# Channel attention on one core: new load pieces in the first pass, and another order of the first stores and reads of the second

## The chip, the cores and the metric

The kernel runs on one core of a Trainium2 chip. The core's engines are TensorE (PE in the profile; its weight loads are PEld), VectorE (DVE), ScalarE (ACT), GpSimd (POOL) and SyncE (SP). Here SP issues all reads from device memory and ACT issues all stores; both go to the core's 16 DMA engines. The metric is device time in microseconds: before the change a median of 733.99 us over 3 runs (733.06 to 737.35). Less is better.

## The reference

`x` has 384 x 384 pixels of 384 channels in bfloat16, 113.25 MB; `w1` is 384 x 96 and `w2` is 96 x 384. Cut to what matters:

```python
xf = x.reshape(B, H * W, C)
gap = jnp.mean(xf, 1)          # mean of each channel
gmp = jnp.amax(xf, 1)          # maximum of each channel
h_a = relu(gap @ w1)
h_m = relu(gmp @ w1)
scale = sigmoid(h_a @ w2 + h_m @ w2)
return x * scale[:, None, None, :]
```

Nothing can be stored before all of `x` has been read once: the scale depends on every pixel.

## The kernel before

The 147,456 pixels lie as 1,152 rows on each of 128 partitions; a row is one pixel's 384 channels, 768 bytes on a partition and 98,304 bytes over all of them. A block of n rows gives each partition n pixels that lie together in memory. All amounts below are in rows.

The first pass reads all 1,152 rows and makes two things of them: running maxima in an accumulator `acc` of eleven rows (DVE, function `larger`, line 311), and sums by TensorE with a column of ones (`sums`, line 274). The second pass multiplies every row by the scale (`multiply`, line 430) and stores it. What doesn't stay on the chip has to be read a second time: 804 rows in nineteen blocks (`AGAIN`) and the accumulator's eleven.

Three slots of 44 rows (`x_88`, `x_89`, `x_90` in the profile; slots 0, 1 and 2) take the loads. `FILLS` names in order what goes into them: a fill has packed pairs (16 rows each) and plain pieces, and the fills go round the slots. Nine pairs, 144 rows, are packed by ACT and PE into three quarters of their size in `room` (function `pack`, lines 316 to 349; ACT lines 321, 324, 339, 341, 344 and 346, PE line 334) and stay there; in the second pass `unpack` (lines 457 to 479, ACT line 464, DVE lines 467 and 470) restores them. The last loads stay as they are: `STAYING`, 44 rows in each slot in the pieces named, 35 rows in `room` itself (`ROOM_PIECES`, loaded ahead of slot `ROOM_LOADS`), and ten in `late` (`LATE_PIECES`, placed among the loads of slot `LATE_AT[0]` after `LATE_AT[1]` of its pieces). Sixteen rows are kept in PSUM. While packing goes on, the first rows of `room` are its scratch, so that the room's loads wait for the last packing.

SP issues the first pass's loads in the order of the list (line 369). A load waits until DVE, PE and, for a pair, ACT have done with the rows that stood in its place; those behind it on SP wait too. `FOLDS` says with how many loads left the accumulator is folded to six and to three rows, so that little is left to fold after the last load; from then on the maxima go in operations of at most three rows (`PARTS`).

Between the passes come the last folds, the means, the transposes of the maxima, the two small products and the sigmoid (lines 297 to 425), and the accumulator's rows are read again (`refill`, line 410).

The second pass has an order written out by hand for SP, ACT and DVE. `order` starts with the three slots; the room is put in at place `ROOM_TURN`. For each block in turn `put` multiplies it and stores it, in the pieces of `FIRST_STORES` for the first ones and whole for the rest; the accumulator's two stores come ahead of piece `ACC_STORES_AT` of the first block. `read_into` takes the next block of `AGAIN` into a slot, in the pieces of `FIRST_READS` for the first two, and adds it to the order. Before the change slots 0 and 1 are read into after two blocks have been put (`LEAD`), slot 2 after four. SP issues these reads (line 454), each when the store of the rows in its place has landed. From the fifth block on, one packed group is unpacked after each.

Of the kernel before, what the change touches and what calls it, by code (L numbers as in the profile page):

```python
# [19 lines left out]
NS = 3  # L20
# [34 lines left out]

PSUM_PIECES = (4, 12)
FILLS = (
    ((16,), ()), ((), (44,)), ((), (44,)), ((16,), ()), ((), (44,)), ((), (44,)),
    ((16,), ()), ((), (44,)), ((), (44,)), ((16,), ()), ((), (44,)), ((), (44,)),
    ((16,), ()), ((), (44,)), ((), (44,)), ((16,), ()), ((), (43,)), ((), (40,)),  # L60
    ((), (36,)), ((), (36,)), ((16,), (27,)), ((), (28,)), ((), (28,)), ((16,), (26,)),
    ((), (24,)), ((), (23, 21)), ((16,), (16,)), ((), (16,)),
)
ROOM_PIECES = (10, 9, 5, 6, 5)
STAYING = ((17, 15, 12), (11, 11, 11, 11), (6, 4, 3, 4, 3, 6, 3, 3, 3, 6, 3))
ROOM_LOADS = 2
LATE_AT = (2, 1)
LATE_PIECES = (5, 5)

FOLDS = {7: 6, 1: 3}  # L70

AGAIN = (44,) * 18 + (12,)
FIRST_STORES = ((1, 2, 3, 4, 4, 6, 8, 8, 8), (8, 8, 9, 9, 10), (10, 11, 14))
FIRST_READS = ((8, 8, 8, 10, 10), (44,))
LEAD = 2
ROOM_TURN = 2
ACC_STORES_AT = 3
ACC_STORES = ((6, 11), (0, 6))
UNPACK_FROM = 4
# [6 lines left out]
def kernel(  # L86
# [20 lines left out]
    def part(ap, block, lo, hi):  # L107

        first, n = block
        return ap[first * P:(first + n) * P, :].rearrange("(p n) c -> p n c", n=n)[:, lo:hi, :]  # L110
# [103 lines left out]
    def packed_place(k):  # L214

        if k < EARLY:
            return early_b, k * PACKED
        if k < N_PACK - EARLY:
            return packed_b, k * PACKED
        return packed_b, (k - N_PACK + EARLY) * PACKED  # L220
# [8 lines left out]
    done, k = A, 0  # L229
    for i, (packs, pieces) in enumerate(FILLS):  # L230
        buf, at = slots[(i - len(FILLS)) % NS], 0
        for m in packs:
            assert m == PAIR
            block, j = packed_place(k)
# [10 lines left out]
    def pieces_of(block, pieces, buf):  # L245
        j = 0
        for m in pieces:
            loads.append((block, j, j + m, buf, j, ()))
            j += m
        assert j == block[1]  # L250

    for s, pieces in enumerate(STAYING):
        if s == ROOM_LOADS:
            pieces_of(room_b, ROOM_PIECES, room)
        n = len(loads)
        pieces_of(stay_b[s], pieces, slots[s])
        if s == LATE_AT[0]:
            j = 0
            for i, m in enumerate(LATE_PIECES):
                loads.insert(n + LATE_AT[1] + i, (late_b, j, j + m, late, j, ()))  # L260
                j += m
# [95 lines left out]
    def fold(n, to):  # L357
        while n > to:
            h = min(n // 2, n - to)
            larger(acc[:, 0:h, :], acc[:, 0:h, :], acc[:, n - h:n, :])  # L360
            n -= h
        return n
# [3 lines left out]
    for i, (block, lo, hi, buf, at, groups) in enumerate(loads):  # L366
# [14 lines left out]
        if i == len(PSUM_PIECES):  # L381
# [5 lines left out]
            continue  # L387
        if n_loads - i in FOLDS:
            width = fold(width, FOLDS[n_loads - i])
            parts, turn = PARTS[width], 0  # L390
        j = 0
# [36 lines left out]
    def multiply(dst, src):  # L428
        n = dst.shape[1]
        nc.vector.tensor_tensor(  # L430
            out=dst, in0=src, in1=scale_bc.unsqueeze(1).to_broadcast([P, n, C]), op=ALU.mult
        )
# [6 lines left out]
    def put(block, buf, pieces, acc_at=None):  # L439
        j = 0  # L440
        for i, m in enumerate(pieces):
            if i == acc_at:
                put_acc()
            rows = buf[:, j:j + m, :]
            multiply(rows, rows)
            nc.scalar.dma_start(out=part(orr, block, j, j + m), in_=rows)
            j += m
        assert j == block[1]
# [8 lines left out]
    def unpack(k):  # L457
        low, code = planes(k)
        j = packed_place(k)[1]
        rows = room[:, j:j + PACKED, :]  # L460
        words = rows.bitcast(U16)
        bits = acc[:, 0:PACKED, :].bitcast(U16)
        more = acc[:, PACKED:PACKED + n_grp, :].bitcast(U16)
        nc.scalar.activation(out=words, in_=low, func=ACT.Copy, bias=float(HIGH))  # L464

        def field(out, shift, op, mask):
            nc.vector.tensor_scalar(out=out, in0=code, scalar1=shift, scalar2=mask, op0=op, op1=ALU.bitwise_and)  # L467

        def add(out, a, b):
            nc.vector.tensor_tensor(out=out, in0=a, in1=b, op=ALU.bitwise_or)  # L470

        for r in range(GROUP - 1):
            field(bits[:, r * n_grp:(r + 1) * n_grp, :], 4 * r, ALU.logical_shift_left, HIGH_BITS)
        last = bits[:, PACKED - n_grp:PACKED, :]
        field(more, 12, ALU.logical_shift_left, 0x8000)
        field(last, 4, ALU.logical_shift_right, 0x0700)
        add(last, last, more)
        add(words, words, bits)
        multiply(rows, rows)

    order = [(b, s) for s, b in enumerate(stay_b)]
    order.insert(ROOM_TURN, (room_b, None))
    stores, reads = list(FIRST_STORES), list(FIRST_READS)
    n_turns = len(order) + len(again)

    def read_into(s):
        if s is None or not again:
            return
        block = again.pop(0)
        get(block, slots[s], reads.pop(0) if reads else (block[1],))  # L490
        order.append((block, s))

    room_left, j = [], EARLY * PACKED
    for m in ROOM_STORES:
        room_left.append((j, j + m))
        j = (j + m) % packed_b[1]
    assert j == EARLY * PACKED

    def put_room(count):
        for _ in range(count):  # L500
            lo, hi = room_left.pop(0)
            nc.scalar.dma_start(out=part(orr, packed_b, lo, hi), in_=room[:, lo:hi, :])
# [5 lines left out]
    while k < len(order):  # L508
        block, s = order[k]
        buf = room if s is None else slots[s]  # L510
        put(block, buf, stores.pop(0) if stores else (block[1],), None if k else ACC_STORES_AT)
        k += 1
        if k == LEAD:
            for j in range(k):
                read_into(order[j][1])
        elif k > LEAD:
            read_into(s)
        if k > UNPACK_FROM and unpacked < N_PACK:
            unpack(unpacked)
            unpacked += 1  # L520
            if unpacked == EARLY:
                nc.scalar.dma_start(out=part(orr, early_b, 0, early_b[1]), in_=room[:, 0:early_b[1], :])
        if k == n_turns - 2:
            put_room(1)
        elif k == n_turns - 1:
            put_room(2)
            multiply(late, late)
            nc.scalar.dma_start(out=part(orr, late_b, 0, LATE_ROWS), in_=late)
# [48 lines left out]
```

## Time and profile before

| | |
|---|---|
| Median of 3 runs | 733.99 us (733.06 to 737.35) |
| The profiled run's own time | 734.48 us |
| Its span, from the first instruction to the last | 732.6 us |
| Read from and written to device memory | 193.51 MB, 113.25 MB |
| Mean rate over the span | 419 GB/s |
| DVE busy | 556.5 us (76%) |
| ACT busy | 250.8 us (34%) |
| PE busy, weight loads | 162.8 us (22%), 52.0 us (7%) |
| First multiply of the second pass starts | 280.36 us |

In the profile a group of instructions is named by its line, engine, operation and what it writes and reads; "x8" is how many, then come the busy time, the mean of one in ns, and the idle time of the engine before them with what ended it. In the timeline the first two numbers of a row are its start and its length in us, and the bracket at the end is the idle time ahead of it. The page's slices cut the span in 40 parts of 18.3 us. The stretches give, for a window in us, the busy time and number of instructions of PE, PEld, DVE, ACT and POOL, the granted clock of PE, the DMA share and the rate in GB/s. In the rows on DMAs the last number is the median time in us from issue to landing, and KB is the size of one; 4224 KB are 44 rows, 1536 KB are sixteen.

### The profile page before, as it was taken

The page shows a single profiled execution, that of the slowest core. Times are in us where ns is not written, and L with a number is a line of the kernel's source. Part 1 is how long each engine was busy: PE and PEld are TensorE (multiplying, and loading weights), DVE is VectorE, ACT ScalarE, POOL GpSimd, SP SyncE. Part 2 cuts the span into 40 slices and gives each one's busy share as a digit, 9 for nine tenths or more (in the row PEclk, how much of TensorE's full clock was granted, in tenths as well). Part 3 has the DMA queues.
Part 4 walks back from the last instruction along what each step waited for, and adds up shares of the span by engine and source line. Part 5 has one row for each costly group of instructions (what it writes and reads, how often), then busy time and mean ns, then how long its engine had stood idle before and what let it go on. Part 6 is the DMA issues. An engine that isn't in the chain of part 4 may idle for free.

```text
span 732.6 us, 3124 instructions
## 1 busy us (share of the span) xinstructions
PE 162.8 (22%) x1069; PEld 52.0 (7%) x1078; DVE 556.5 (76%) x422; ACT 250.8 (34%) x135; POOL 0.7 (0%) x6
## 2 busy tenths in 40 slices
PE   3664656554756561000000000000000000000000
PEld 0221212111211120000000000000000000000000
DVE  6689989899999998979276777277667666667930
ACT  4998889853997400002011011011110011111100
POOL 0000000000000000000000000000000000000000
PEclk9968878677675755555555555555555555555555
DMA  9999999999999988999999999999999999999997
GB/s 378 440 431 414 431 415 412 400 426 427 427 424 422 417 329 306 386 442 425 437 439 424 435 436 441 421 437 440 424 437 437 423 437 439 423 437 427 434 438 339
DMA packets 19391, 306.95 MB, mean 419 GB/s; under 512 B 2512, under 2 KB 3120, under 8 KB 8368
## 3 DMA queue, kind: packets, MB, share of 16 engines
q1 hardware_dynamic: 12896, 193.52, 62.5%
q10 hardware_dynamic: 6480, 113.25, 36.2%
q8 instruction: 8, 0.13, 0.1%
q14 instruction: 7, 0.06, 0.0%
HBM read 193.51 MB, written 113.25 MB: 419 GB/s over the span
## 4 chain that ended last, share of the span: by engine, by line
DMA 58%; DVE 34%; issue 2%; ACT 0%; SPq 0%; PE 0%; DVEq 0%; ACTq 0%
DMA x<-in_x_dram 37%; DMA out_dram<-x 21%; DVE hole L311 20%; DVE x L430 12%; DVE room L430 1%; DVE hole L430 1%; ACT room L464 0%; SPq L369 0%; DVE room L470 0%; DVEq L535 0%; PE bank_a L424 0%; ACT scale_bc L425 0%; DVE small L419 0%; PE bank_a L418 0%; PE bank_a L422 0%
## 5 line engine op out<-in xcount | busy, mean ns | idle before, releaser
L430 DVE TENSOR_TENSOR x<-x,scale_bc 128x16896 bf16<-128x16896 bf16 (+9 forms) x34 | 191.5, 5660 | 94.6 <-DMA x<-in_x_dram 93.5
L311 DVE TENSOR_TENSOR hole<-hole,x 128x1920 bf16<-128x1920 bf16 (+2 forms) x211 | 235.7, 1191 | 20.0 <-DMA x<-in_x_dram 18.6
L464 ACT ACTIVATE room<-room 128x3072 uint16<-128x3072 uint8 x18 | 49.7, 2763 | 360.2 <-DVE x L430 309.4
L274 PE MATMUL bank_a<-x,small 128*1 128x512 bf16 (+1 forms) x816 | 92.7, 481 | 49.4 <-DMA x<-in_x_dram 48.6
L334 PE MATMUL bank_b<-room 128*128 128x512 bf16 x153 | 59.9, 526 | 51.9 <-ACT room L324 22.4
L321 ACT CAST room<-x 128x3072 bf16<-128x3072 uint8 x18 | 48.7, 2750 | 45.1 <-DMA x<-in_x_dram 45.1
L339 ACT COPY room<-x 128x3072 uint8<-128x3072 uint8 x18 | 49.3, 2737 | 0.0
L470 DVE TENSOR_TENSOR room<-room,hole 128x3072 uint16<-128x3072 uint16 x18 | 31.6, 1758 | 23.0 <-ACT room L464 23.0
L341 ACT ACTIVATE room<-room,w_sb 128x6144 uint8<-128x6144 bf16 x9 | 48.7, 5407 | 0.0
L430 DVE TENSOR_TENSOR room<-room,scale_bc 128x3072 bf16<-128x3072 bf16 (+3 forms) x21 | 38.9, 1861 | 0.6
L274 PEld LDWEIGHTS <-small 128*1 128x1 bf16 x861 | 29.1, 95 | 131.8 <-issue 116.0
L467 DVE TENSOR_SCALAR hole<-room 128x768 uint16<-128x768 uint16 x90 | 25.7, 353 | 0.0
L346 ACT ACTIVATE room<-room,w_sb 128x3072 bf16<-128x3072 uint16 x9 | 25.7, 2853 | 0.0
L334 PEld LDWEIGHTS <-room 128*128 128x128 bf16 x162 | 19.0, 119 | 90.9 <-issue 85.7
L344 ACT ACTIVATE room<-bank_b 128x512 uint16<-128x512 f32 x27 | 15.9, 590 | 1.7 <-PE bank_b L334 1.7
L324 ACT ACTIVATE room<-x 128x1536 bf16<-128x1536 bf16 x9 | 13.3, 1478 | 0.0
L470 DVE TENSOR_TENSOR hole<-hole 128x768 uint16<-128x768 uint16 x18 | 10.0, 558 | 0.6
L299 ACT COPY w_sb<-bank_a 65x128 f32<-65x128 f32 x2 | 0.5, 262 | 25.3 <-PE bank_a L274 24.8
L311 DVE TENSOR_TENSOR hole<-hole,room 128x1920 bf16<-128x1920 bf16 (+2 forms) x7 | 7.6, 1152 | 0.0
L379 DVE COPY kept_ps<-x 128x768 uint32<-128x768 uint32 (+1 forms) x2 | 3.5, 1760 | 4.2 <-DMA x<-in_x_dram 4.2
L274 PE MATMUL bank_a<-room,small 128*1 128x512 bf16 (+1 forms) x27 | 4.1, 543 | 4.2 <-DMA room<-in_x_dram 4.2
L311 DVE TENSOR_TENSOR hole<-hole 128x1920 bf16<-128x1920 bf16 (+2 forms) x6 | 4.9, 823 | 0.1
(46 smaller groups left out, 29.8 us busy)
## 6 DMA issues: line engine op xcount, KB each, us to landing
x<-in_x_dram SPq DMA_DIRECT2D x27, 4224.0 KB, 24.4
out_dram<-x ACTq DMA_DIRECT2D x19, 4224.0 KB, 24.0
x<-in_x_dram SPq DMA_DIRECT2D x11, 1536.0 KB, 12.2
x<-in_x_dram SPq DMA_DIRECT2D x2, 3456.0 KB, 16.7
out_dram<-room ACTq DMA_DIRECT2D x2, 3072.0 KB, 31.4
x<-in_x_dram SPq DMA_DIRECT2D x2, 2688.0 KB, 16.7
x<-in_x_dram SPq DMA_DIRECT2D x4, 1056.0 KB, 11.4
out_dram<-room ACTq DMA_DIRECT2D x1, 4224.0 KB, 29.5
```

The source lines that it names most:

```text
L274: nc.tensor.matmul(sum_ps[q * QP:q * QP + 1, 0:g * P], lhsT=ones_bf[:, 0:1], rhs=rows[:, :, q * P:(q + 1) * P], start=(summed == 0), stop= ...
L311: nc.vector.tensor_tensor(out=out, in0=a, in1=b, op=ALU.max)
L321: nc.scalar.copy(out=lanes[:, h], in_=halves[:, h, :, :, 1].rearrange("p (w g) c -> p w (g c)", g=n_grp))
L334: nc.tensor.matmul(pack_ps, lhsT=diag[:, w, :], rhs=flat(src)[:, i * 512:(i + 1) * 512], start=(w == 0), stop=(w == len(WEIGHTS) - 1),)
L339: nc.scalar.copy(out=planes(k + i)[0], in_=halves[:, i, :, :, 0])
L341: nc.scalar.activation(out=flat(test).bitcast(U8), in_=flat(high), func=ACT.Abs, bias=middle, scale=1.0 / STEP)
L344: nc.scalar.activation(out=code[:, i * 512:(i + 1) * 512], in_=pack_ps, func=ACT.Copy, bias=-OFFSET)
L346: nc.scalar.activation(out=flat(test), in_=flat(test).bitcast(U16), func=ACT.Square, bias=good, accum_out=flags[:, k // 2:k // 2 + 1],)
L430: nc.vector.tensor_tensor(out=dst, in0=src, in1=scale_bc.unsqueeze(1).to_broadcast([P, n, C]), op=ALU.mult)
L464: nc.scalar.activation(out=words, in_=low, func=ACT.Copy, bias=float(HIGH))
L467: nc.vector.tensor_scalar(out=out, in0=code, scalar1=shift, scalar2=mask, op0=op, op1=ALU.bitwise_and)
L470: nc.vector.tensor_tensor(out=out, in0=a, in1=b, op=ALU.bitwise_or)
```

## The change

Only constants and the condition that starts the reads change; the work and the bytes read and stored are the same.

In the first pass most fills with a pair now have a plain piece as well, of 12 to 28 rows; there are 25 fills instead of 28, with the same nine pairs and 804 plain rows. All pairs now go into slot 2, and it is refilled every third time. The room, the staying rows and the late rows come in other pieces; the late rows are one piece of ten and are read among the loads of slot 1 instead of slot 2. The accumulator is folded to six rows with nine loads left instead of seven.

In the second pass the room is stored second, after slot 0, instead of third. The first block goes in seven pieces that begin with four rows, instead of nine that begin with one; slot 1 goes in three pieces instead of five, slot 2 in two (20 and 24) instead of whole. No read starts before three blocks have been put; then slot 1 is read into first, in pieces of 20 and 24, and slot 0 after it, whole.

```diff
 FILLS = (
-    ((16,), ()), ((), (44,)), ((), (44,)), ((16,), ()), ((), (44,)), ((), (44,)),
-    ((16,), ()), ((), (44,)), ((), (44,)), ((16,), ()), ((), (44,)), ((), (44,)),
-    ((16,), ()), ((), (44,)), ((), (44,)), ((16,), ()), ((), (43,)), ((), (40,)),
-    ((), (36,)), ((), (36,)), ((16,), (27,)), ((), (28,)), ((), (28,)), ((16,), (26,)),
-    ((), (24,)), ((), (23, 21)), ((16,), (16,)), ((), (16,)),
+    ((16,), ()), ((), (40,)), ((), (44,)), ((16,), (28,)), ((), (44,)), ((), (44,)),
+    ((16,), (28,)), ((), (43,)), ((), (27,)), ((16,), (27,)), ((), (44,)), ((), (44,)),
+    ((16,), (28,)), ((), (36,)), ((), (40,)), ((16,), (20,)), ((), (36,)), ((), (32,)),
+    ((16,), (28,)), ((), (27,)), ((), (28,)), ((16,), (24,)), ((), (23, 21)), ((), (20,)),
+    ((16,), (12, 16)),
 )
-ROOM_PIECES = (10, 9, 5, 6, 5)
-STAYING = ((17, 15, 12), (11, 11, 11, 11), (6, 4, 3, 4, 3, 6, 3, 3, 3, 6, 3))
+ROOM_PIECES = (8, 6, 5, 6, 5, 5)
+STAYING = ((16, 14, 14), (11, 11, 11, 6, 5), (4, 4, 3, 3, 6, 6, 3, 3, 6, 3, 3))
 ROOM_LOADS = 2
-LATE_AT = (2, 1)
-LATE_PIECES = (5, 5)
+LATE_AT = (1, 3)
+LATE_PIECES = (10,)
 
-FOLDS = {7: 6, 1: 3}
+FOLDS = {9: 6, 1: 3}
 
-FIRST_STORES = ((1, 2, 3, 4, 4, 6, 8, 8, 8), (8, 8, 9, 9, 10), (10, 11, 14))
-FIRST_READS = ((8, 8, 8, 10, 10), (44,))
-LEAD = 2
-ROOM_TURN = 2
+FIRST_STORES = ((4, 4, 4, 7, 8, 8, 9), (10, 12, 13), (13, 15, 16), (20, 24))
+FIRST_READS = ((20, 24), (44,))
+FIRST_INTO = (2, 0)
+ROOM_TURN = 1
...
-        if k == LEAD:
-            for j in range(k):
+        if k == NS:
+            for j in FIRST_INTO:
                 read_into(order[j][1])
-        elif k > LEAD:
+        elif k > NS:
             read_into(s)
```

`FIRST_INTO` counts places in `order`, which then holds slot 0, the room, slot 1 and slot 2: place 2 is slot 1, place 0 is slot 0.

## The prediction

> **What bounds the kernel now.** I read the page's slices first, then stretches of them, then the waits, and last DVE and the loads in the first pass.
>
> ```profile
> span 732.6 us, 3124 instructions
> ...
> GB/s 378 440 431 414 431 415 412 400 426 427 427 424 422 417 329 306 386 442 425 437 439 424 435 436 441 421 437 440 424 437 437 423 437 439 423 437 427 434 438 339
> ...
> DMA 58%; DVE 34%; issue 2%; ACT 0%; SPq 0%; PE 0%; DVEq 0%; ACTq 0%
> ```
>
> Except at the turn between the passes (slices 15 to 17) and at both ends, the transfers run at 400 to 440 GB/s; the chain that ended last is DMA and DVE alone. The bytes are the same after the change, so only stretches below the best rate can give time back. The next lines are such stretches; their last two columns are DMA share and GB/s.
>
> ```profile
> 20.00:150.00 130.00, 78.42 (x489) 25.18 (x495) 114.32 (x98) 116.38 (x60) 0.00 (x0) 0.77 1.00 418
> 150.00:240.00 90.00, 55.07 (x363) 16.74 (x365) 89.23 (x83) 66.57 (x34) 0.00 (x0) 0.73 1.00 425
> ...
> 270.00:282.00 12.00, 6.14 (x63) 4.03 (x59) 9.88 (x19) 1.78 (x7) 0.00 (x0) 0.50 0.47 153
> 282.00:297.00 15.00, 0.00 (x0) 0.00 (x0) 15.00 (x11) 0.00 (x0) 0.00 (x0) 0.50 0.98 393
> 297.00:304.00 7.00, 0.00 (x0) 0.00 (x0) 7.00 (x5) 0.00 (x0) 0.00 (x0) 0.50 1.00 329
> 304.00:690.00 386.00, 0.00 (x0) 0.00 (x0) 268.59 (x163) 49.52 (x18) 0.00 (x0) 0.50 1.01 433
> 690.00:733.00 43.00, 0.00 (x0) 0.00 (x0) 11.32 (x5) 0.22 (x1) 0.00 (x0) 0.50 0.91 390
> ```
>
> From 304 to 690 the second pass runs at 433 throughout: nothing to win there. The first pass is slower in 20:150, with 44-row loads, than in 150:240, with loads of 16 to 40 rows, though bigger pieces should be no worse. DVE's timeline says where it is lost: each row opens when a 44-row load lands.
>
> ```profile
> 23.23 9.44 DVE L311 TENSOR_TENSOR hole<-hole,x 128x2304 bf16<-128x2304 bf16 x8 [5.42 <-DMA x<-in_x_dram]
> 33.26 12.85 DVE L311 TENSOR_TENSOR hole<-hole,x 128x2304 bf16<-128x2304 bf16 x11 [0.59 <-DMA x<-in_x_dram]
> 48.32 9.44 DVE L311 TENSOR_TENSOR hole<-hole,x 128x1920 bf16<-128x1920 bf16 x8 [2.21 <-DMA x<-in_x_dram]
> 58.36 12.84 DVE L311 TENSOR_TENSOR hole<-hole,x 128x1920 bf16<-128x1920 bf16 x11 [0.60 <-DMA x<-in_x_dram]
> 72.19 9.44 DVE L311 TENSOR_TENSOR hole<-hole,x 128x2304 bf16<-128x2304 bf16 x8 [0.98 <-DMA x<-in_x_dram]
> 82.55 12.85 DVE L311 TENSOR_TENSOR hole<-hole,x 128x2304 bf16<-128x2304 bf16 x11 [0.92 <-DMA x<-in_x_dram]
> 96.26 9.44 DVE L311 TENSOR_TENSOR hole<-hole,x 128x1920 bf16<-128x1920 bf16 x8 [0.86 <-DMA x<-in_x_dram]
> 107.40 12.85 DVE L311 TENSOR_TENSOR hole<-hole,x 128x1920 bf16<-128x1920 bf16 x11 [1.70 <-DMA x<-in_x_dram]
> 121.11 9.44 DVE L311 TENSOR_TENSOR hole<-hole,x 128x2304 bf16<-128x2304 bf16 x8 [0.86 <-DMA x<-in_x_dram]
> 131.78 12.84 DVE L311 TENSOR_TENSOR hole<-hole,x 128x2304 bf16<-128x2304 bf16 x11 [1.23 <-DMA x<-in_x_dram]
> 147.10 33.30 DVE L311 TENSOR_TENSOR hole<-hole,x 128x1920 bf16<-128x1920 bf16 x30 [2.48 <-DMA x<-in_x_dram]
> ```
>
> Intervals over one 44-row load: 10.03, 10.04, 10.36, 11.14, 10.67. Over a pair and a 44-row load: 15.06, 13.83, 13.71, 13.71, 15.32 (the last with 43 rows). Clean values are 10.03 and 13.71, so a 16-row load takes 3.68, a row (10.03 - 3.68) / 28 = 0.227 us, and each load 0.05 us besides. Over clean the ten intervals are long by 0.01 + 0.33 + 1.11 + 0.64 + 1.35 + 0.12 + 1.84 = 5.4 us. DVE does 44 rows in 9.44 us, less than 10.03, and waits at each of them: it isn't the cause. The issues are:
>
> ```profile
> x<-in_x_dram SPq DMA_DIRECT2D x8, 4224.0 KB, 15.0
> ...
> x<-in_x_dram SPq DMA_DIRECT2D x5, 1536.0 KB, 15.9
> ```
>
> The first line is of 20:150, the second of 150:270: a 44-row load lands 15.0 us after its issue and needs 10.03 itself, so it was queued only 5.0 us ahead. Later a 16-row load is queued 15.9 - 3.7 = 12.2 us ahead. In both stretches the DMA view counts four packets of kind "instruction" on q8, each of which holds one of the 16 DMA engines for about 1 us; only with the short queue is the pass below its rate. I read it so: one engine is held, the others finish their shares, find nothing queued and stop until SP may issue again.
>
> **The change part by part.**
>
> *Fills.* A slot with a packed pair now also takes 20 to 28 rows in most cases: 25 fills instead of 28, and 64 loads in the first pass instead of 60. A 44-row load then has a pair and up to 28 rows before it in SP's queue, 28 x 0.227 = 6.4 us more: a lead of about 11 us instead of 5. Of the 5.4 us lost, between none and all come back; by the nearest rows, those of 150:240 (425 GB/s, against 418 over 130 us: 2.1 us) and the clean 430 GB/s that 60 rows in 13.71 make (3.6 us), I take half, **-2.7**. Four more loads at 0.05: **+0.2**. The pair's load, which SP issues in order, waits for ACT to let go of the previous pair, and behind it now stand its 28-row neighbour and the next slots. ACT lets go some 12.6 us after a pair has landed (13.14 to 25.70 in the trace), and the next pair comes after 83 to 116 more rows, 19 to 26 us: covered, by 6 us at the least; without the cover SP would stand for the difference. PE's sums of the neighbour stand between the pair's packing matmuls; they wait for a landing 6.4 us after the pair's, and the second packing group needs ACT's 10.1 us: covered. DVE has 130 - 114.3 = 15.7 us idle in 20:150, so it follows a faster queue. Against the change speaks that the transfers fade out over 270 to 274 us, so that some engine is behind the others by then, while five of the ten intervals are clean, which a single slow engine would also give. The Trainium skill, page "DMA: Bandwidth & Descriptors", section "Latency and other measured facts", says that DMA engines 7 and 15 are usually slower than the rest. By that rule a longer queue would gain nothing and the sum would be -1.4; by the row of 150:240, with its longer queue and higher rate, it is the sum below. The trace doesn't number its engines and can't show which.
>
> *End of the first pass.* Room's loads wait for the last packing; SP issues them from 242.9, 12 us before they land, and 205 rows follow the last pair instead of 209, so that it comes 0.9 us later: nothing. Late's ten rows move before the room, in one load: nothing. Folding to six rows at nine loads left instead of seven makes nine more rows go in three-row operations, net 0.67 a piece against 2.34 for 11 rows: **+0.1**. The last loads are again 12 rows, and after them the same folds, transposes and sigmoid.
>
> *First stores.* The first multiply is of four rows (0.95 us) instead of one (0.36): the first store is issued 0.6 us later, at 281.35. Before, the first 55 rows, in eleven stores, had landed at 296.45. After: the one-row store landed 1.67 after its issue, so four rows need 1.67 + 3 x 0.227 = 2.35, and 51 rows in eight pieces 51 x 0.227 + 8 x 0.05 = 12.0 behind it, since DVE (4 rows per 0.87) stays ahead of 0.96: 281.35 + 2.35 + 12.0 = 295.7. **-0.7**; bound on the other side +0.6, if only the delay counts.
>
> *The first reads.* In 297:304, where the five 8- and 10-row reads start beside 8- and 9-row stores, the rate is 329: 7 x (1 - 329 / 425) = 1.6 us lost. Now the reads start after 134 rows are stored, at about 283.7 + 130 x 0.227 + 0.6 = 313.8 instead of 296.5, in pieces of 20 and 24 beside stores of 20 and 24. Nothing shows that start; the 44-row read at 346.5 in the chain starts beside 44-row stores with no dip in the slices. Between -1.6 and +1.6 (the same dip, once for each slot): I take **-0.8**. SP has slot 1's read ahead of slot 0's, which is free earlier; the third slot's 44 rows of stores, 10 us, keep the queues full meanwhile. Three instead of five slot-1 stores, two instead of five reads, one more for the third slot: four DMAs fewer at 0.05, **-0.2**.
>
> *The room second.* ACT's first unpacking waited for the room's store (50.7 us, one wait); that store lands earlier and the wait goes. The transfers ran at 433 throughout it: nothing, and reads' landings are what is late next.
>
> The sum: -2.7 + 0.2 + 0.1 - 0.7 - 0.8 - 0.2 = **-4.1 us**. The profiled run took 734.48 (span 732.6), 0.49 above the median 733.99; the sum shortens either alike: 730.4 against that run, **729.9** against the median.
>
> **Rivals.**
>
> *One engine is the last all along* (22%). Then a longer queue lets only the others run ahead. For it is the fading out at 270 to 274, against it the five intervals that are long by different amounts, between 0.1 and 1.8 us. Nothing of the 2.7 comes: 729.9 + 2.7 = 732.6. The rule of the skill's page above would be one way to it.
>
> *All comes back* (12%): -5.4 and -1.6 instead of -2.7 and -0.8 gives 726.4.
>
> *The reads start badly and the first store's delay stays* (10%): with +1.6, +0.6 and no gain in the fills, 733.99 + 0.2 + 0.1 + 0.6 + 1.6 - 0.2 = 736.3.
>
> *The late reads bunch the slots* (8%; slower). If the third slot's stores land before slots 1 and 0 are read, no store is queued while DVE multiplies: one multiply of 8.96 us and 1.67 from issue to landing, 10.6 idle. It decides when DVE needs longer for a slot (8.96) than the reads still queued (10.03 for 44 rows). 733.99 - 2.7 + 0.3 + 10.6 = 742.2. Against it: before, the chain has a store of 29.00 us from 317.45 on and then a read, a similar bunch, and 304:690 still ran at 433.
>
> **How the numbers follow.** The forecast has the other 48%, with 727.5 to 732 as its own range, so the time is 729.9. From 726.8 to 736.4 lie the forecast, the first and third rivals and a little of the second, over 8 in 10. 1%, about what a measurement of this kernel can tell from no change, is 7.3 us: below 726.65 lie most of "all comes back" and a rest, 0.11; above 741.3 the last rival and things unseen, 0.10; 0.79 between.
>
> **What would show it.** Right: 20:150 at 424 GB/s or more, 44-row loads landing 18 us or more after issue, DVE's intervals near 0.228 us a row; the first multiply of the second pass 2 to 3 us before 280.36; no stretch near 315 at 329. Wrong: 418 again with the longer queue (first rival); first multiply not earlier; a stretch of low DMA share between 320 and 370 (the last).

## The result, and the profile after

The changed kernel takes a median of 730.34 us over 5 runs (730.17 to 732.20). The kernel before, run beside it, takes 734.33 (733.06 to 737.35). The ratio is 0.9957, with a 95% interval of 0.9941 to 0.9973: 3.2 us faster by the ratio (2.0 to 4.3), 4.0 by the medians. The forecast was 729.9, within 1%. The profiled run of the changed kernel took 730.17 us, 4.3 less than the profiled run of before.

The first lines are from the page of the changed kernel: the span, the rate in 40 slices and the shares of the chain that ended last.

```profile
span 728.4 us, 3125 instructions
...
GB/s 384 426 439 415 430 444 416 432 429 424 429 423 423 416 312 355 424 391 441 431 431 445 416 440 442 419 445 427 434 438 424 444 425 436 434 427 428 439 431 351
...
DMA 57%; DVE 20%; ACT 15%; issue 2%; PE 1%; SPq 0%; ACTq 0%; DVEq 0%
```

The sixth to eighth slices, 415, 412 and 400 before, are 444, 416 and 432. At the turn between the passes 329 and 306 have become 312 and 355, as the first pass ends earlier; the start of the reads, which was in the slice of 386 before, is now one slice later, in that of 391. ACT has come into the chain, but not as a new bound: the chain now follows a packed pair through its packing to the next pair's load, while DMA is busy throughout.

The same stretches of the changed kernel as were shown of before:

```profile
20.00:150.00 130.00, 73.75 (x510) 23.87 (x517) 118.59 (x105) 101.76 (x52) 0.00 (x0) 0.81 1.00 429
150.00:240.00 90.00, 54.39 (x344) 16.57 (x343) 89.13 (x83) 83.43 (x41) 0.00 (x0) 0.75 1.01 426
270.00:282.00 12.00, 2.99 (x48) 2.19 (x47) 9.88 (x15) 0.83 (x3) 0.00 (x0) 0.50 0.65 230
282.00:297.00 15.00, 0.00 (x0) 0.00 (x0) 15.00 (x8) 0.00 (x0) 0.00 (x0) 0.50 1.03 423
297.00:304.00 7.00, 0.00 (x0) 0.00 (x0) 7.00 (x3) 0.00 (x0) 0.00 (x0) 0.50 1.02 427
304.00:690.00 386.00, 0.00 (x0) 0.00 (x0) 268.41 (x166) 49.73 (x18) 0.00 (x0) 0.50 1.00 431
```

20:150 went from 418 to 429 GB/s, and 150:240 stayed (425 and 426). 130 us at 418 would be 126.7 at 429: 3.3 us. The first multiply of the second pass says the same for the whole first pass, here in the DVE timeline of the changed kernel:

```profile
276.31 2.69 DVE L430 TENSOR_TENSOR x<-x,scale_bc 128x1536 bf16<-128x1536 bf16 x3 [1.17 <-ACT scale_bc L425]
```

It starts at 276.31 instead of 280.36, 4.05 us earlier. From there to the end of the span are 452.1 us, against 452.2 before. So between these two executions everything was won in the first pass, and the second pass, for which the prediction had 1.7 us, gave nothing. Two more views show how. First the DMA view of 20:150 (packets, MB and their share of the time of 16 engines; then the loads), then the DVE timeline where it opens with a 44-row load that follows another 44-row load:

```profile
q8 instruction: 4, 0.07, 0.2%
...
x<-in_x_dram SPq DMA_DIRECT2D x4, 4224.0 KB, 21.4
x<-in_x_dram SPq DMA_DIRECT2D x3, 2688.0 KB, 21.9
x<-in_x_dram SPq DMA_DIRECT2D x5, 1536.0 KB, 14.8
```

```profile
53.77 9.44 DVE L311 TENSOR_TENSOR hole<-hole,x 128x1920 bf16<-128x1920 bf16 x8 [2.58 <-DMA x<-in_x_dram]
63.79 18.79 DVE L311 TENSOR_TENSOR hole<-hole,x 128x1920 bf16<-128x1920 bf16 x16 [0.58 <-DMA x<-in_x_dram]
...
109.79 9.44 DVE L311 TENSOR_TENSOR hole<-hole,x 128x2304 bf16<-128x2304 bf16 x8 [1.96 <-DMA x<-in_x_dram]
119.82 26.54 DVE L311 TENSOR_TENSOR hole<-hole,x 128x2304 bf16<-128x2304 bf16 x24 [0.59 <-DMA x<-in_x_dram]
```

A 44-row load lands 21.4 us after its issue instead of 15.0 and still needs 10 itself, so that it is queued 11 us ahead, as the prediction had it. Both intervals shown are clean: 10.02 and 10.03 us for 44 rows. The four packets of kind "instruction" are still there (0.2% of 16 engines' 130 us, about 1 us of one engine for each); they no longer show in the rate.

### The profile page after: what moved, and what is told of

It reads as the page before. It is cut to its first block, busy times and chain, and to the rows that moved or that the text cites. A ratio compares the mean times of both kernels' runs of the same rounds, so it can differ in the third digit from the quotient of the medians.

```text
span 728.4 us, 3125 instructions
## 1 busy us (share of the span) xinstructions
PE 157.0 (22%) x1069; PEld 50.8 (7%) x1078; DVE 556.4 (76%) x423; ACT 250.3 (34%) x135; POOL 0.7 (0%) x6
## 4 chain that ended last, share of the span: by engine, by line
DMA 57%; DVE 20%; ACT 15%; issue 2%; PE 1%; SPq 0%; ACTq 0%; DVEq 0%
DMA x<-in_x_dram 39%; DMA out_dram<-x 19%; DVE x L430 13%; ACT room L321 6%; ACT room L339 6%; DVE hole L311 5%; ACT room L324 2%; ACT room L464 1%; DVE room L430 1%; DVE room L470 1%; ACT room L344 1%; DVE hole L430 1%; PE bank_b L334 0%; SPq L369 0%; ACTq L446 0%
## 5 line engine op out<-in xcount | busy, mean ns | idle before, releaser
L430 DVE TENSOR_TENSOR x<-x,scale_bc 128x16896 bf16<-128x16896 bf16 (+10 forms) x31 | 191.3, 6195 | 94.6 <-DMA x<-in_x_dram 93.4
L311 DVE TENSOR_TENSOR hole<-hole,x 128x1920 bf16<-128x1920 bf16 (+3 forms) x215 | 235.8, 1174 | 16.1 <-DMA x<-in_x_dram 14.6
L274 PE MATMUL bank_a<-x,small 128*1 128x512 bf16 x816 | 95.7, 494 | 62.2 <-DMA x<-in_x_dram 61.4
L334 PE MATMUL bank_b<-room 128*128 128x512 bf16 x153 | 52.6, 468 | 41.3 <-ACT room L324 19.3
L334 PEld LDWEIGHTS <-room 128*128 128x128 bf16 x162 | 17.2, 110 | 76.9 <-issue 69.4
L311 DVE TENSOR_TENSOR hole<-hole,room 128x2304 bf16<-128x2304 bf16 (+2 forms) x7 | 7.6, 1155 | 0.0
L311 DVE TENSOR_TENSOR hole<-hole 128x384 bf16<-128x384 bf16 (+4 forms) x6 | 4.9, 823 | 0.1
```

The lines of the kernel that those rows point to most:

```text
L274: nc.tensor.matmul(sum_ps[q * QP:q * QP + 1, 0:g * P], lhsT=ones_bf[:, 0:1], rhs=rows[:, :, q * P:(q + 1) * P], start=(summed == 0), stop= ...
L311: nc.vector.tensor_tensor(out=out, in0=a, in1=b, op=ALU.max)
L334: nc.tensor.matmul(pack_ps, lhsT=diag[:, w, :], rhs=flat(src)[:, i * 512:(i + 1) * 512], start=(w == 0), stop=(w == len(WEIGHTS) - 1),)
L430: nc.vector.tensor_tensor(out=dst, in0=src, in1=scale_bc.unsqueeze(1).to_broadcast([P, n, C]), op=ALU.mult)
```

## The experiments

Each kernel was timed in five rounds beside the kernel before. Ratios are to that kernel in the same rounds, with the 95% interval; the changed kernel's own is 0.9957 [0.9941, 0.9973]. The median of the kernel before was 734.33 beside the changed kernel, and 733.48, 734.22 and 733.98 in the three later sets of rounds.

### Which part of the change does it

**The new fills alone**, in the kernel before (the diff of `FILLS` as shown with the change, nothing else).

> The kernel before with the new list of fills alone (25 fills, pairs that share their slots, 64 loads). Theory, short queue: the first pass lost time because a 44-row load stood only 5.0 us ahead in its queue while an engine was held by an instruction packet; with some 11 us ahead this goes. Expected 730.0 to 730.8 us, 3.5 to 4.3 below before; 20:150 at 427 GB/s or more; first multiply of the second pass near 276.5 instead of 280.36; the dip of 329 GB/s where the reads start stays, shifted with it. Rival, the ends: the gain comes from the end of the first pass and the turn, so that this kernel is within 1.0 us of before (733.3 or more) and 20:150 reads 418 to 421.

Measured: 731.07 us, ratio 0.9961 [0.9947, 0.9976], or 2.9 us faster. The stretch 20:150:

```profile
20.00:150.00 130.00, 75.39 (x512) 23.89 (x514) 118.29 (x105) 102.34 (x53) 0.00 (x0) 0.80 1.00 428
```

428 GB/s, and the first multiply starts at 276.6. The median is 0.3 us above what was expected of the theory and far from the rival's 733.3. The profiled run, at 734.24, was the longest of its six; it lost in the second pass what the first had won (455.9 us from the first multiply to the end of the span, against 452.2 before, at 431 GB/s instead of 434 in the last 330). Why single executions do that is not known.

**The changes of the second pass alone**:

```diff
-FIRST_STORES = ((1, 2, 3, 4, 4, 6, 8, 8, 8), (8, 8, 9, 9, 10), (10, 11, 14))
+FIRST_STORES = ((4, 4, 4, 7, 8, 8, 9), (10, 12, 13), (13, 15, 16), (20, 24))
...
-ROOM_TURN = 2
+ROOM_TURN = 1
...
-        if k == LEAD:
+        if k == NS:
```

> The kernel before with the second pass's changes alone (first stores, first reads, place of the room, the start of the reads after three blocks). Theory: its terms came to nothing in the changed kernel (the first 55 rows' stores landed 16.06 us after the first multiply against 16.09, one dip of 1.6 us took the place of another), so within 0.7 us of before: 733.6 to 735.0. Rival, by the terms as predicted (-0.7, -0.8, -0.2): 732.6.

Measured: 733.90 us, ratio 1.0002 [0.9990, 1.0015]: nothing, and 1.7 us less (0.9977) lies outside the interval. Here the prediction's terms for the second pass, taken together, fall.

**The end of the first pass alone** (room, staying and late pieces, `FOLDS`):

```diff
-STAYING = ((17, 15, 12), (11, 11, 11, 11), (6, 4, 3, 4, 3, 6, 3, 3, 3, 6, 3))
+STAYING = ((16, 14, 14), (11, 11, 11, 6, 5), (4, 4, 3, 3, 6, 6, 3, 3, 6, 3, 3))
...
-FOLDS = {7: 6, 1: 3}
+FOLDS = {9: 6, 1: 3}
```

> The kernel before with the changed end of the first pass alone (pieces of the room and of the staying rows, late rows in one load, folding to six rows at nine loads left). Theory: nothing that can be seen, 733.7 to 734.8; the last landing of the first pass stays within 0.5 us of 274.03. Rival: the end of the pass is where the gain is made (20:150 alone gave 3.5 us in the traces, so at most 1 us is left for it): 733.3 or less.

Measured: 734.45 us, ratio 1.0016 [1.0000, 1.0032]: no gain, and perhaps a loss.

**The changed kernel with the old fills**, the same question from the other side:

> The changed kernel with the old list of fills; everything else as changed. Theory, short queue: the loss comes back whole, 733.8 to 734.8 us, 3.5 to 4.3 above the changed kernel, and 20:150 reads 418 to 420 GB/s. Rival, the ends: it keeps at least half the gain, 732.3 or less.

Measured: 733.84 us, ratio 0.9996 [0.9983, 1.0010]. Without the new fills all else that was changed is worth nothing. Its stretch reads as before:

```profile
20.00:150.00 130.00, 77.76 (x496) 24.82 (x496) 113.71 (x97) 116.18 (x60) 0.00 (x0) 0.79 0.99 416
```

How far two traces of the same loads differ can be read here too. The kernel before, the second pass alone, the end alone and this kernel load the same rows in 20:150, and read 418, 420, 423 and 416 GB/s there; their first multiplies start at 280.36, 280.11, 278.26 and 280.27. With the new fills (the changed kernel, the fills alone and the next kernel) the rates are 429, 428 and 428, and the first multiplies start at 276.31, 276.56 and 276.36. The two groups don't overlap, but a single trace with the old fills is good to some 4 GB/s and 2 us only.

**The changed kernel with the old pieces at the end of the first pass** (the diff of the third run, backwards), since that run left open whether the new pieces cost something:

> The changed kernel with the old pieces at the end of the first pass (room, staying rows, late rows, folding at seven loads left); new fills and new second pass. Theory, these pieces do nothing: 729.8 to 731.2 us. Rival, by the run of these pieces alone (1.2 us above the kernel before, interval 0 to 2.4): they cost, and this kernel beats both, 728.6 to 729.6 us.

Measured: 730.32 us (730.17 to 730.44), ratio 0.9944 [0.9925, 0.9963]; the changed kernel had 730.34. They do nothing that can be seen.

### Why the fills help

**The longer queue by another way**: pairs keep their slots to themselves, but the plain loads are halved, so that the first half of a slot is free earlier.

```diff
-    ((16,), ()), ((), (44,)), ((), (44,)), ((16,), ()), ((), (44,)), ((), (44,)),
+    ((16,), ()), ((), (22, 22)), ((), (22, 22)), ((16,), ()), ((), (22, 22)), ((), (22, 22)),
...
```

> The kernel before with each of the first ten plain 44-row fills read as two loads of 22 rows; pairs still have their slots alone, ten more loads. Theory, short queue: the first half of a slot is free earlier, so loads stand some 10 us ahead, and most of the loss in 20:150 goes although no slot is shared: 20:150 at 425 GB/s or more, 730.5 to 732.3 us (3.5 back at the most, less 10 x 0.05 for the loads). Rival, sharing: what counts is that a pair no longer keeps a slot to itself, so that this kernel stays within 1 us of before, 418 to 420 GB/s.

The DMA view and the stretch of 20:150:

```profile
q8 instruction: 4, 0.07, 0.2%
...
x<-in_x_dram SPq DMA_DIRECT2D x16, 2112.0 KB, 18.2
```

```profile
20.00:150.00 130.00, 81.09 (x488) 23.79 (x493) 116.58 (x100) 117.68 (x60) 0.00 (x0) 0.76 1.01 428
```

A 22-row load, 5.0 us long, lands 18.2 us after its issue, so the queue is 13 us deep, and 428 GB/s come without any shared slot. The first multiply starts at 276.89. The traced first pass is as the theory has it. The time is less clear: 732.91 us, ratio 0.9987 [0.9971, 1.0002], 0.6 above the expected range, while the profiled run, at 730.65, was the shortest of twelve. So that trace may flatter this kernel; it speaks for the theory, and does not settle it.

**A smaller dose**: twelve rows beside the pair.

```diff
-    ((16,), ()), ((), (44,)), ((), (44,)), ((16,), ()), ((), (44,)), ((), (44,)),
+    ((16,), ()), ((), (44,)), ((), (44,)), ((16,), (12,)), ((), (44,)), ((), (44,)),
...
-    ((), (36,)), ((), (36,)), ((16,), (27,)), ((), (28,)), ((), (28,)), ((16,), (26,)),
-    ((), (24,)), ((), (23, 21)), ((16,), (16,)), ((), (16,)),
+    ((), (32,)), ((), (32,)), ((16,), (27,)), ((), (24,)), ((), (20,)), ((16,), (18,)),
+    ((), (20,)), ((), (16, 15)), ((16,), (16,)), ((), (12,)),
```

> The kernel before with 12 rows beside the pair in five fills, where the changed kernel has up to 28: a dose between the two, the 44-row loads 12 x 0.227 = 2.7 us further ahead, 7.7 instead of 5.0. Theory, short queue: a part of the gain, 20:150 at 420 to 425 GB/s and 731.3 to 733.0 us. Rival, a threshold: nothing under about 10 us ahead, 733.2 or more; other rival, sharing as such: the whole gain, 731 or less.

Measured: 735.33 us, ratio 1.0016 [1.0006, 1.0027], slower, against every expectation. The stretches and then the longest of SP's waits from 140 to 280 show where the gain is lost:

```profile
20.00:150.00 130.00, 74.83 (x519) 24.78 (x525) 118.09 (x104) 107.55 (x55) 0.00 (x0) 0.79 1.00 428
150.00:236.00 86.00, 48.30 (x322) 14.99 (x325) 83.40 (x78) 69.77 (x37) 0.00 (x0) 0.74 0.99 416
236.00:266.00 30.00, 15.06 (x121) 4.76 (x120) 28.90 (x28) 12.06 (x9) 0.00 (x0) 0.77 0.99 398
```

```profile
SPq L369 <- DVE hole L311: 62.2, 17, 9.7
SPq L369 <- ACT room L339: 28.0, 4, 12.6
```

With twelve rows (44-row loads landing after 17.0 us, 7 us ahead) 20:150 has the whole gain already, 428. It is given back from 150 on (416 and 398, against 426 and 414 before). The five times twelve rows are missing there, and I had put the last three pairs closer together, with 71 and 69 plain rows between them, where the kernel before has 83 or more. SP now stands up to 12.6 us for ACT to let go of a pair (9.1 before), and the loads behind it stand too. So the cover of a pair's load, for which the prediction had counted on 83 rows or more, is the likely reason; a run with the pairs further apart wasn't made. It explains the lost gain and not the rest: the first multiply starts at 280.00, still 0.36 us earlier than before. The traced run, at 738.38, was the longest of its twelve, and its other 4.4 us lie in the second pass (456.6 us from the first multiply to the end of the span, against 452.2), whose program is that of before. Why the median lies above that of before is open.

**No instruction packets**: the kernel before without TensorE's column sums, which leaves the mean out but for its last rows.

```diff
-        for r in to_sum[i]:
-            sums(buf[:, r[0]:r[1], :], TOT - tail_rows)
```

> The kernel before without TensorE's column sums in the first pass (the mean is left out but for its last rows), so that PE has far fewer instructions; fills, loads, maxima and the second pass are as before. Theory: the loss in 20:150 comes of instruction packets that hold one DMA engine for 1 us each while the queue is short; with fewer of them it goes although the queue stays short: 0 or 1 such packets in 20:150 instead of four, 424 GB/s or more, 730.5 to 732 us. Rival, the short queue loses of itself (the issue and the landing of a load leave gaps whatever the packets do): 418 to 421 GB/s as before, 733 or more.

Measured: 730.54 us, ratio 0.9950 [0.9923, 0.9978]. The DMA view and the stretch of 20:150:

```profile
q8 instruction: 1, 0.02, 0.1%
...
x<-in_x_dram SPq DMA_DIRECT2D x8, 4224.0 KB, 14.2
```

```profile
20.00:150.00 130.00, 40.88 (x102) 12.89 (x104) 118.17 (x101) 118.73 (x61) 0.00 (x0) 0.61 1.00 429
```

The queue is as short as before (14.2 us from issue to landing), the fills are the old ones, and the rate is 429. The short queue loses nothing of itself; the sums, and with them three of the four packets, are needed for the loss. That it is the packets, and not something else that the sums do, this run can't tell.

**The changed kernel without the sums** (the same two lines; the same part is left out):

> The changed kernel without TensorE's column sums (the mean is left out but for its last rows), as was done to the kernel before, which then took 730.54 us. Theory, packets alone: without them the longer queue has nothing to cover, so both lists of fills give the same: 729.8 to 731 us, 20:150 at 428 to 430 GB/s. Rival, the new list helps in another way too: 727 to 729 us.

Measured: 730.37 us (730.27 to 730.50), ratio 0.9945 [0.9927, 0.9964], 429 GB/s. Without the sums the new fills have nothing to win.

**Twice the packets**, in both kernels: the sums in matmuls of two rows.

```diff
-MM_ROWS = 4
+MM_ROWS = 2
```

> The kernel before with the column sums in matmuls of two rows instead of four, so that PE has about twice as many instructions for them; work, fills and loads are the same. Theory, instruction packets under a short queue: some 16 such packets in the first pass instead of 8, and the loss doubles: 20:150 at 408 to 413 GB/s, 736.5 to 738.5 us. Rival, PE becomes late and holds the slots: the same rise with the changed fills too. Rival, packets do nothing: 733.5 to 734.5.

> The changed kernel with the same: sums in matmuls of two rows, about twice as many instruction packets, under the longer queue. Theory: the queue covers them, 20:150 at 426 GB/s or more, 730.0 to 731.3 us, at most 1 above the changed kernel. Rival, PE becomes late: it rises as much as the kernel before does, 2 us or more.

Measured: 735.22 us, ratio 1.0018 [1.0000, 1.0036], with the old fills, and 731.55 us, ratio 0.9974 [0.9954, 0.9995], with the new ones. The first line is 20:150 of the one, the second of the other:

```profile
20.00:150.00 130.00, 77.47 (x879) 38.14 (x883) 114.23 (x98) 114.89 (x59) 0.00 (x0) 0.75 0.99 413
```

```profile
20.00:150.00 130.00, 70.52 (x930) 38.17 (x940) 118.24 (x105) 102.05 (x53) 0.00 (x0) 0.83 1.00 428
```

With seven packets instead of four the new fills keep their 428, as the theory has it. That the old fills lose more isn't shown. Their 413 lies 3 GB/s under the lowest of the four traces with four packets (416 to 423), and the load that lands at 147.10 in the kernel before lands at 147.19 here, where twice the loss would have put it some 5 us later. The total rises by some 1.2 us in both kernels (735.22 against 733.98 for the kernel before in the same rounds, 731.55 against 730.34), less than expected for the one and a little more for the other, so that the time doesn't tell the theory from its rival, a late PE. What speaks against that rival is that SP in 20:150 waits for DVE and ACT alone with the old fills, and only 0.4 us for PE with the new ones. In the changed kernel the rise comes at the very end of the first pass: the first multiply is at 277.71 instead of 276.31, and three instruction packets lie in 236 to 280 instead of one. That few loads are left there to queue behind a held engine may be the reason; no run tried it. PE is not late there; its last sums still wait for a load:

```profile
268.72 0.59 PE L274 MATMUL bank_a<-x,small 128*1 128x256 bf16 x6 [0.35 <-DMA x<-in_x_dram]
```

**Where the packets lie.** The traces settle more than the rates do. Take the ten intervals between landings from 23 to 147 us, as the prediction did, in this trace with the old fills and the other five of them (before, the second pass alone, the end alone, the old fills in the changed kernel, no sums), and let the DMA view count the packets of each. Of these 60 intervals 24 hold a packet. Fifteen are 0.75 us or more over the prediction's clean values, and all fifteen hold one; the other nine packets lie in intervals that are 0.4 us over at most. Where a packet moves, a long interval moves with it: the first interval holds one with doubled packets alone, and takes 11.37 us there, against 10.02 to 10.04 in the other five. In the kernel before, the three longest (those from 33.26, 96.26 and 131.78, over by 1.35, 1.11 and 1.84) hold three of the four packets. The kernel without sums has one packet, and it falls between these two rows, 10.85 us apart instead of 10.03, the only one of its ten intervals that is over by more than 0.5:

```profile
118.92 9.44 DVE L311 TENSOR_TENSOR hole<-hole,x 128x2304 bf16<-128x2304 bf16 x8 [0.87 <-DMA x<-in_x_dram]
129.77 12.85 DVE L311 TENSOR_TENSOR hole<-hole,x 128x2304 bf16<-128x2304 bf16 x11 [1.41 <-DMA x<-in_x_dram]
```

So with the short queue a long interval has a packet, but a packet doesn't always make one: with twice the packets four of the seven cost 0.4 us at most, and the ten intervals are over by 5.5 us in all, against 5.4 before.

Put together (median us; GB/s in 20:150; instruction packets on q8 in it):

| | no sums, 1 packet | four rows, 4 packets | two rows, 7 packets |
|---|---|---|---|
| old fills | 730.54; 429 | 734.33; 418 (four traces: 416 to 423) | 735.22; 413 |
| new fills | 730.37; 429 | 730.34; 429 | 731.55; 428 |

### The start of the reads

**One read instead of three** in the changed kernel: slot 1 whole, slot 0 one block later.

```diff
-FIRST_READS = ((20, 24), (44,))
-FIRST_INTO = (2, 0)
+FIRST_READS = ((44,), (44,))
+FIRST_INTO = (2,)
...
+        if k == NS + 1:
+            read_into(order[0][1])
```

> The changed kernel with one read at the start of the reads instead of three: slot 1 whole (44 rows), and slot 0 only after the next block has been put. Theory, a burst: the dip to 356 GB/s at 308 to 318 comes of several reads that are issued at once, as before the change, while the lone 44-row read at 346.5 of the kernel before had none; so the dip goes: 420 GB/s or more in that stretch, 1.0 to 1.6 us below the changed kernel, 729 to 729.5 us. Rival, the turn: it comes of the first read among stores alone, so it stays with 1 to 1.6 us lost, 730.0 to 731 us.

Measured: 735.26 us, ratio 1.0020 [1.0009, 1.0031]: 5 us above the changed kernel, outside both expectations. First the stretches of the changed kernel, then of this one:

```profile
308.00:318.00 10.00, 0.00 (x0) 0.00 (x0) 5.17 (x2) 0.00 (x0) 0.00 (x0) 0.50 1.01 356
318.00:330.00 12.00, 0.00 (x0) 0.00 (x0) 0.00 (x0) 0.00 (x0) 0.00 (x0) 0.50 1.00 426
330.00:345.00 15.00, 0.00 (x0) 0.00 (x0) 11.27 (x8) 2.76 (x1) 0.00 (x0) 0.50 1.01 436
```

```profile
308.00:318.00 10.00, 0.00 (x0) 0.00 (x0) 5.00 (x2) 0.00 (x0) 0.00 (x0) 0.50 1.01 370
318.00:330.00 12.00, 0.00 (x0) 0.00 (x0) 0.00 (x0) 0.00 (x0) 0.00 (x0) 0.50 1.00 422
330.00:345.00 15.00, 0.00 (x0) 0.00 (x0) 12.27 (x8) 2.76 (x1) 0.00 (x0) 0.50 0.92 347
```

The dip at 308:318 stays with a single read (370 against 356), so a burst of reads isn't what makes most of it; it comes with the first read among stores. At 330:345 the share falls to 0.92 and the rate to 347: with slot 0's read later the queues run thin there, some 3 us. From 345 to 500 the rate is 430 against 434, about 1.4 us more. Together they are the loss: from the first multiply, at 276.14, to the end of the span are 456.6 us, against 452.1. The early reads of the changed kernel keep the queues full, whatever their start costs.

## Why the prediction was right, and where it was not

*The mechanism.* Its two conditions are shown. A longer queue (the new fills, the halved loads, the twelve rows, 7 us ahead or more) brings 20:150 to 428 or 429, and so does leaving the sums out with the queue left short. In the same rounds the latter is worth 734.22 - 730.54 = 3.7 us under the short queue, with seven packets fewer in the first pass, and under the long one nothing. That it is their packets is shown by where the long intervals lie, but not by their number: twice as many lost no more. The last step, that the others finish their shares, find nothing queued and stop, is not shown. The trace doesn't number the engines, and the DMA share of 20:150 reads 1.00 in both kernels, where idle engines for 3.3 of 130 us would leave 0.97. The share is no exact measure (1.05 in one of the ten intervals), so this doesn't refute it either. What the engines do in the lost time, and why some packets cost nothing, is open.

The Trainium skill, page "Runtime: NRT & Kernel Launch", section "Instruction fetch mechanics", says that a sequencer fetches its instructions in blocks of 16 KiB, 256 instructions, through a DMA queue of its own, at a cost mostly hidden. The traces agree with the size (four packets are 0.07 MB) and about with the number (3,124 - 1,391 instructions fewer without the sums, seven packets fewer: 248 each). The page's "mostly hidden" doesn't hold for the time of this kernel with the old fills, if the packets are what the sums' 3.7 us are; with the new fills it holds.

*Fills, -2.7, and four loads, +0.2*: -2.5 was forecast, and the new fills alone measured -2.9 (-1.8 to -3.9). I had taken half of the 5.4 us that the long intervals add up to; 20:150 gave 3.3 in the trace, near the 3.6 that the clean 430 GB/s made, and the first multiply came 4.05 us earlier, where 2 to 3 had been named as the sign. The clean intervals were the better row than 150:240.

*One engine is the last all along* (22%) fell: nothing would have come of the fills. The row of the Trainium skill, page "DMA: Bandwidth & Descriptors", section "Latency and other measured facts", on engines 7 and 15, weighed in the prediction, was read too widely: its best guess at a cause is one that it calls "SWDGE-specific" (for descriptors written by software), while the profile's page names both data queues of this kernel hardware_dynamic. No run shows an effect like it, though without numbered engines no trace can exclude it.

*All comes back* (12%): the trace gave 3.3 of the 5.4 us in the fills, and none of the 1.6 us of the reads.

*First stores, -0.7*: this step failed. Before, the first 55 rows' stores had landed 16.09 us after the first multiply, after it 16.06. The duration was at fault, as the DMA view of the changed kernel from 276 to 330 shows:

```profile
out_dram<-x ACTq DMA_DIRECT2D x3, 384.0 KB, 3.4
```

I had four rows land 2.35 us after their issue, from the one-row store's 1.67 and the steady rate per row. The first of the three took 3.34, and the view of before already had four-row stores at 3.3. The delay of the first store, 0.6, and this 1.0 took back what fewer pieces saved.

*First reads, -0.8*: this failed as well. The dip was not half as deep but the same: 10 x (1 - 356 / 426) = 1.6 us at 308:318, where before it was 1.6 at 297:304. My row for a good start, the 44-row read at 346.5 before, was no first read among stores; the run with one read shows that the number of reads matters little (370 GB/s against 356).

*Fewer DMAs, -0.2*: not seen, and too small to be seen by itself; the whole second pass differs by 0.1 to 0.2 us between the two traces.

*The end of the first pass, +0.1*: right; with the old pieces back the time is the same to 0.02 us. *The room second, 0*, wasn't run by itself; the second pass as a whole gave nothing.

*The late reads bunch the slots* (8%): nothing of it; 318:330 and 330:345 run at 426 and 436.

So the sum, -4.1, came out at -3.2 to -4.0, depending on the measure, but its parts were shared out wrongly: the fills gave more than their term, and the second pass gave none of its 1.7. That the median of 730.34 lies so near the forecast of 729.9 is in part luck: the fills won as forecast but somewhat more, and the second pass nothing of what it was to win. By ratios, the fills alone (0.9961), the second pass alone (1.0002) and the end alone (1.0016) make 0.9979, while all together make 0.9957. The intervals are too wide to say whether the parts help each other. One observation speaks for it: the kernels with both new fills and new second pass mostly repeat within a few tenths (730.17 to 730.44 for the one with the old end pieces; 730.17 to 730.34 for the changed kernel, but for one run at 732.20), where the new fills with the old second pass go from 730.03 to 734.24. Why is open.

## What to carry to other kernels

When a kernel is bound by transfers, compare the rate of its stages: one that runs below a stage with smaller pieces may be short of queued work, and issue-to-landing minus a load's own length says how far ahead its loads are queued. Some 1,700 instructions of PE for the sums (3,124 in all against 1,391 without) came with a slower stream of loads here where 5 us were queued ahead, and not where 7 us or more were. When part of such a list is shortened, see that what stands between two uses of a scarce buffer stays as long as its release takes.

## What was not expected of the hardware

The instruction packets are 0.13 MB of the 113 MB of the first pass, and the sums that bring seven of the eight cost 3.7 us under the short queue, about as long as 1.6 MB of loads would take at 429 GB/s. And the first read among stores costs some 1.6 us of transfer, with five reads at 297:304, with three at 308:318, and some 1.2 with one (370 against 422 GB/s), while the DMA share stays at 1.0: the engines count as busy and move less. What they do in that time the trace doesn't show.
